# Attention with a gated MLP on one core: early first keys, 64-row pairs, and the output copy on VectorE

## Chip, core and metric

One of the eight cores of a Trainium2 chip. The metric is device time in microseconds of one execution. Engines: TensorE (PE; its weight loads are PEld), VectorE (DVE), ScalarE (ACT), GpSimd (POOL) and SyncE (SP, which here only issues DMAs).

## The reference

```python
xn  = layernorm(A_x)                             # (2048, 512)
q, k, v = split(xn @ A_wqkv)                     # 32 heads of 16
p   = softmax(q @ k.T * 16**-0.5, axis=-1)       # 32 x 2048 x 2048
s   = concat(p @ v) @ A_wo
g   = silu(gelu(xn @ B_w1 + B_b1) @ B_w2 + B_b2) # hidden 1376
out = A_x + s * g
```

## The kernel before

Projections and MLP are made of two-part numbers: every float32 operand is split into a rounded high part and the rest, and a product takes three matmuls (high x high, high x low, low x high). q and k go out to DRAM as qk_h and qk_l and come back in the layout of the scores. A group is 4 heads (8 groups); a unit is one group and one chunk of 512 queries (32 units, u = 4 x group + chunk).

TensorE runs most matmuls as row tiles: a matmul that contracts over 64 rows or fewer takes rows 0 to 63 or 64 to 127 of the array, and two of them, one in each row tile (the code's `a` is 0 or 1), run at once. All instructions are placed by hand; each engine takes its own in the order of the program.

Softmax needs the row maximum before the exponential. So each unit is scored twice. An **S tile** (`s_mm`, L178) is 128 queries x 512 keys of one head into a PSUM bank, and VectorE takes its maxima (`s_max`, L184); 64 of them make a unit, 2,048 in all, and behind a unit come a reduce over its maxima (nm, L239), a split on GpSimd and a transpose (mh, L258) that goes to DRAM. A **T tile** (`t_one`, L710) is 128 keys x 512 queries, with the maxima as two more rows of the contraction, and ScalarE's exponential (L712) carries it to SBUF. A **V** (`pv_step`, L775) multiplies the four heads' exponentials of 128 keys with v, into the one bank of `ps_v`, over 16 steps of a unit; then the bank is copied to `os` (L782) and moved, divided and used.

The **first part** (to about 476 us) computes layernorm, q, k and v, and the MLP. At its start, transposes (`turn`, L422), v tiles (`v_tile`, L79) and the q and k of groups 0 and 1 (`q_first`, L438) are full-array matmuls of 128 rows. From 52 us on everything runs in `run()` (L561) as pairs of 64 rows, one in each row tile. `fill()` puts S tiles between them once row `FILL0` of this counting is reached, spread evenly over the rows: 4 x `LEAD` = 576 of them. S tiles alternate between the banks `ps_a` and `ps_b`.

The **second part** runs 512 steps, 16 to a unit; step n makes the T tiles of step n and the V of step n-1:

```python
ORDER = {0: "TTTTV", 3: "TSXTTSTYV"}
def due(n):
    return min(4 * L, 4 * LEAD + max(0, 3 * n - 1))
```

The difference of `due` is the number of S tiles in a step: three till they run out, at n = 491, and none afterwards. X and Y are two half tiles, one in each row tile, that share a bank: X (256 keys) is written first, a token through the POOL queue (L216) tells that it is done, then Y follows and one maximum covers both. S tiles use three banks here (`ps_a`, `ps_b`, `ps_x`), T tiles four. From n = 492 the output projections of finished tokens run in the steps as well.

Keys lie in three buffers (`KB`, group g in buffer g % 3): one from the start (kt0), one where v's weights were (kt1), one in two of the slots of the normalized x. The keys of group 0 come in by chunks (`load_k`) when kt0 is free, the queries of unit 0 and 1 by `load_qs` into qz0 and qz1.

Of the kernel before, what the change touches and what calls it, by code (L numbers as in the profile page):

```python
# [8 lines left out]
F32 = mybir.dt.float32  # L9
# [7 lines left out]
P = 128  # L17
# [12 lines left out]
EPS = 1e-5  # L30
SCALE = DH ** -0.5
VW = DH + 1
LEAD = 144
NW = 10
EARLY = 4
DONE = 492
FILL0 = 38
HB = 4
W2B = 2
ORDER = {0: "TTTTV", 3: "TSXTTSTYV"}  # L40
HC = CH // 2
KB = 3
XB = 6
BANKS = ("ttvt", "xtmt", "ttvt")

# [2 lines left out]
def fused(ctx: ExitStack, tc: tile.TileContext, x, wqk, wv, wo, w1, b1, w2, b2, out):  # L48
# [50 lines left out]
        return src[r0:r0 + 48, c0:c0 + n].rearrange("(p d) s -> d p s", d=DH)[:, 0:3:2, :]  # L99

    def load_k(g, pieces=range(6), eng=nc.sync, c0=0, n=S):
        both = kws[g % KB]
        for i in pieces:
            a, b = divmod(i, 3)
            r, cs = slice(64 * a + DH * b, 64 * a + DH * b + DH), slice(c0, c0 + n)
            src = rows((qk_h, qk_h, qk_l)[b], g, 1, a, c0, n)
            if both is not None:
                eng.dma_start(both[r, :, cs].bitcast(F32), src)
            else:
                for p in range(2):  # L110
                    eng.dma_start(kts[g % KB][p][r, cs].bitcast(F32), src[:, p])

    def k_ones(kt):
        for p in range(2):
            for a in range(2):
                nc.sync.dma_start(kt[p][64 * a + 48:64 * a + 50].bitcast(F32), ones_d)

    def new_k(pool):
        both = pool.tile([P, 2, S], F32R, name=f"kt{len(kts)}")
# [46 lines left out]

    def at_of(job):
        u, st, p = job
        return divmod(st, NCH) if u % (NCH * KB) else divmod(st, NCH)[::-1]

    def s_mm(ps, job, a, c0, k0, w):
        u, st, p = job
        qi, ki = at_of(job)
        if u not in MX:
            MX[u] = qring.tile([P, GH, NCH, NCH, 2], F32, name="mx")
        r = slice(64 * a, 64 * a + 3 * DH)
        k0 += ki * CH
        return nc.tensor.matmul(ps[:, c0:c0 + w], QS[u][r, p, qi * P:(qi + 1) * P],  # L178
                                kts[u // NCH % KB][p][r, k0:k0 + w], start=True, stop=True).ins

    def s_max(ps, job, heads, parts):
        u, p = job[0], job[2]
# [81 lines left out]
    xh = [slot(2 * c, (P, KT, CH), F32R) for c in range(NCH)]  # L264
    xl = [slot(2 * c + 1, (P, KT, CH), F32R) for c in range(NCH)]
    wk = sa.enter_context(tc.tile_pool(name="work_a", bufs=2))
    b1_sb = xp.tile([P, FT], F32, name="b1_sb")
    b2_sb = xp.tile([P, D], F32, name="b2_sb")

# [102 lines left out]
    with ExitStack() as s1:  # L372
# [126 lines left out]
        for c in range(1, NCH):  # L499
            for t in range(NCH * c, NCH * c + NCH):  # L500
                turn(t)
            if c < NCH - 1:
                ln(NCH * c + NCH, NCH)
            else:
                nc.scalar.activation(warm[:, 1:], warm[:, :1], AF.Gelu_apprx_tanh)
                w1_load(0)
                w2_load(0)
                w2_load(1)
                break
            v_tile(c - 1)  # L510
            q_first(c)

    keep_r = ctx.enter_context(tc.tile_pool(name="keep_r", bufs=1, side="right"))
    qring = ctx.enter_context(tc.tile_pool(name="qring", bufs=2, side="right"))
# [6 lines left out]
    for i in range(2):  # L521
        qzs.append(qzp.tile([P, 2, CH], F32R, name=f"qz{i}"))

    load_qs(0)
    load_k(0, c0=0, n=CH)
    load_k(0, c0=CH, n=S - 2 * CH)
    v_tile(NCH - 2)
    q_first(NCH - 1)
    v_tile(NCH - 1)
    load_k(0, c0=S - CH, n=CH)  # L530

    prog.update(n=0, pe=0, seen=0)
    writer = {}
    s_when, row = [], [0, 0]
    ndown = sum(1 for e in plan if e[0] == "down")
    ROWS = 12 * (4 * VQ + 2 * len(pairs)) + 6 * ndown - 10 + 2 * LEAD - FILL0

    def fill(a):
        due = FILL0 + sum(made) * ROWS // (4 * LEAD)
# [53 lines left out]

    PH = {}

    def terms(u, a, begin):
        kind, n, f = u
        c = f if kind == "q" else n
        out = []
        for k in range(KT):  # L600
            for i, j in ((0, 0), (0, 1), (1, 0)):
                if kind == "v":
                    lhs, rhs = (xh, xl)[i][c][:, k, f * P:(f + 1) * P], (wv_h, wv_l)[j][:, k]
                else:
                    w = W1[u if kind == "m" else n]
                    lhs, rhs = w[i][:, k * P:(k + 1) * P], (xh, xl)[j][c][:, k]
                out.append([u, PH[u], lhs, rhs, False, False])
        if begin:
            out[0][4] = True
        else:  # L610
            out[-1][5] = True
        return out
# [3 lines left out]
    def down(c, f, part):  # L616
        i = c * FT + f
        if f == 0 and part == 0:
            PA[c] = [ps_v.tile([P, D], F32, name="pv")] + [ps_t.tile([P, D], F32, name="pst") for t in range(3)]
        h, w = HS[c, f], W2[c, f]  # L620
        side = (part + i) % 2
        ops = [[], []]
        for a in range(2):
            for t in ((0, 1), (2, 3))[(a + side) % 2]:
                ts = slice(t * P, (t + 1) * P)
                for n, (x, y) in enumerate(((0, 0), (0, 1), (1, 0))):
                    ops[a].append(((c, t), PA[c][t], h[x][:, ts], w[y],
                                   f == 0 and part == 0 and n == 0, f == FT - 1 and part == 1 and n == 2))
        n = prog["pe"]
        if (c, f, part) == parts[-2]:  # L630
            run(ops, {2: [lambda: mark(True)], 5: [lambda: mark(True)]})
        else:
            run(ops, {3: [lambda: mark_early(n)]})
        if part == 0:
            w2_split(i + 1)
            w2_load(i + 3)
            return
        del HS[c, f], W2[c, f]
        if f == FT - 1:
            for t in (0, 2, 1, 3):  # L640
                gt = wk.tile([P, D], F32, name="gt", bufs=4)
                if c == NCH - 1:
                    nc.vector.tensor_add(gt, PA[c][t], b2_sb)  # L643
                else:
                    nc.scalar.activation(gt, PA[c][t], AF.Copy)
                rs = slice(c * CH + t * P, c * CH + (t + 1) * P)
                if c < NCH - 1:
                    chores.append((gt, rs))
                else:
                    nc.gpsimd.dma_start(g_d[rs, :], gt)  # L650
# [22 lines left out]
    def quad(n, at):  # L673
# [4 lines left out]
        for i in range(at, at + 2):  # L678
# [4 lines left out]
            if i >= 2:  # L683
                for u in (us[i - 2], us[i]):
                    v_out(u[1] * NCH + u[2], PH.pop(u))

    def ask_k(g):
        errands.append((k_ones, kts[g]))
        for i in range(6):
            errands.append((load_k, g, (i,)))  # L690
# [12 lines left out]
    def t_one(u, k, p, a):  # L703
        g = u // NCH
        if (u, k) not in PT:
            PT[u, k] = slot(3 + len(PN) % 3, (P, GH, CH))
            PN.append(1)
        ps = t_tile()
        r = slice(64 * a, 64 * a + 3 * DH + 2)
        nc.tensor.matmul(ps, kts[g % KB][p][r, k * P:(k + 1) * P],  # L710
                         QT[u][r, p, :], start=True, stop=True)
        nc.scalar.activation(PT[u, k][:, 2 * p + a, :], ps, AF.Exp, scale=SCALE)  # L712

    k_ones(kts[0])
    for n, e in enumerate(plan):
        if e[0] == "half":
            half(*e[1:])
        elif e[0] == "first":
            quad(*e[1:])
            if e[1:] == (0, 2):  # L720
                ask_qs(1)
        else:
            if e[1] == parts[-2]:
                nc.scalar.activation(mhw, ident_r[:1, :1].bitcast(F32), AF.Exp)
            if e[1] == parts[-1]:
                for i in range(EARLY):
                    t_one(0, 0, i // 2, i % 2)
            down(*e[1])
# [21 lines left out]
    qts.append(kp.tile([P, 2, CH], F32R, name="qt1"))  # L750
    load_qt(1)
    load_mh(1)
    wo_h = kp.tile([P, KT, D], F32R, name="wo_h")
    wo_l = kp.tile([P, KT, D], F32R, name="wo_l")

    WR = {}

# [11 lines left out]
    def pv_step(u, k):  # L769
# [8 lines left out]
        if k == NT - 1:  # L778
            OS[u] = wb.tile([P, CH], F32, name="os", bufs=1)
            pv = PV.pop(u)  # L780
            if u < NU - 1:
                nc.scalar.activation(OS[u], pv, AF.Copy)  # L782
            else:
                nc.scalar.activation(OS[u][:, :HC], pv[:, :HC], AF.Copy)
                nc.vector.tensor_copy(OS[u][:, HC:], pv[:, HC:])
# [29 lines left out]

    def home(i):
        if i not in homes:
            homes[i] = (slot(i, (P, KT, D)) if i < KB else
                        keep_r.tile([P, 2 * KT, D], F32, name="kt0"))
        return homes[i]  # L820

    def load_gx(t):
# [1 line left out]
        if t < NW and i < 6:  # L824
            GX[t] = wb.tile([P, 2, D], F32, name="gx", bufs=3)
        elif t < NT - NCH:
            GX[t] = home(KB)[:, i - 6 * (t < NW):][:, :2]
        else:
            GX[t] = home(1 + i // KT)[:, i % KT:i % KT + 2]
        nc.sync.dma_start(GX[t][:, 0], g_d[t * P:(t + 1) * P, :])  # L830
# [78 lines left out]
    L = 16 * NU  # L909

    def due(n):
        return min(4 * L, 4 * LEAD + max(0, 3 * n - 1))

    for u in range(NU):
        g, c = divmod(u, NCH)
        if c == 0 and g == KB:
            for i in range(6):
                at(56 + i, load_k, g, (i,), nc.gpsimd, 0, S // 2)
                at(64 + i, load_k, g, (i,), nc.gpsimd, S // 2, S // 2)
        elif c == 0 and g > KB:  # L920
            for i in range(6):
                at(64 * (g - KB + 1) + 6 + i, load_k, g, (i,), nc.gpsimd)
        if u >= 2:
            at(16 * u - 14, load_qt, u)
            need = min(n for n in range(L) if due(n) >= 64 * (u + 1)) + (4 if u < NU - 1 else 2)
# [22 lines left out]
    for i, t in enumerate(late[:2]):  # L948
        at(L - 2 + i, w_token, t)
    for k in range(KT):  # L950
        at(104 + 16 * k, load_wo, k)
        at(110 + 16 * k, wo_high, k)
        at(114 + 16 * k, wo_low, k)
    jobs.extend(heads[made[0]:])
    for n in range(L + 1):
        ua, ka = divmod(n, 16)
# [73 lines left out]
```

## Time and profile before

| | |
|---|---|
| median of 3 runs | 1575.72 us (1575.42 to 1576.03) |
| the profiled execution | 1575.59 us |
| its span, first to last instruction | 1573.8 us, granted clock 0.999 |
| first part, 64-row pairs | 52.56 to 475.6 us |
| first V group of the second part | 477.27 us |
| steps with output projections | from about 1475 us |

In the page, busy time is the union of an engine's instructions; "mean ns" is that of one. The chain of waits follows the end of the program backwards through what released each instruction. A timeline row is a start, a length, engine, line, operation, output and inputs, and a count when neighbours of one kind are merged into a row (the length is then from the first start to the last end); in brackets stands what the engine was idle for.

### The profile page before, as it was taken

What the parts mean: (1) busy time and instruction counts of PE and PEld (TensorE: products, weight loads), DVE (VectorE), ACT (ScalarE), POOL (GpSimd) and SP (SyncE); (2) the same over time, 40 slices, a digit from 0 to 9 for tenths busy, and PEclk for the clock granted to TensorE, in tenths of its full rate; (3) what the DMA queues carried; (4) which work ended last, traced back from release to release, by engine and by line L of the source; (5) the groups of instructions that cost most, each with busy time, mean ns of one, the idle gap of its engine ahead of it and who ended that gap; (6) DMA issues with size and microseconds to landing.
All of it is one profiled execution on the core that took longest, in us unless ns stands there. A gap on an engine that the chain in (4) does not pass through costs nothing.

```text
span 1573.8 us, 32597 instructions
## 1 busy us (share of the span) xinstructions
PE 1561.6 (99%) x12234; PEld 955.1 (61%) x12234; DVE 1376.2 (87%) x2275; ACT 1254.8 (80%) x2516; POOL 378.0 (24%) x398
## 2 busy tenths in 40 slices
PE   8999999999999999999999999999999999999998
PEld 7899999999995444444444444444444444444455
DVE  7499999999998999999999999999999999999733
ACT  4333433434339999999999999999999999999994
POOL 4135575765641001001100200000010000000144
PEclk9999999999999999999999999999999999999999
DMA  6625442454422114111511411221041111111162
GB/s 208 152 60 141 130 139 99 134 155 123 132 84 76 43 30 72 30 36 36 86 31 31 69 37 36 52 51 29 23 79 30 33 29 31 41 29 23 45 210 100
DMA packets 79486, 116.92 MB, mean 74 GB/s; under 512 B 28868, under 2 KB 29124, under 8 KB 78152
## 3 DMA queue, kind: packets, MB, share of 16 engines
q1 hardware_dynamic: 75580, 101.90, 23.9%
q0 software_dynamic: 3264, 12.35, 4.1%
q8 instruction: 96, 1.57, 0.4%
q10 hardware_dynamic: 484, 0.60, 0.1%
q14 instruction: 62, 0.51, 0.1%
HBM read 84.35 MB, written 25.97 MB: 70 GB/s over the span
## 4 chain that ended last, share of the span: by engine, by line
PE 98%; DVE 1%; issue 0%; DMA 0%; ACT 0%; POOL 0%; DVEq 0%
PE pv L775 33%; PE pst L710 16%; PE ps L710 14%; PE ps L561 13%; PE ps L178 9%; PE pst L561 7%; PE pv L561 2%; PE ps L881 1%; PE ps L438 1%; PE ps L79 1%; PE pst L79 1%; DVE st L399 0%; PE pst L422 0%; DMA xt<-in_x 0%; PE pst L438 0%
## 5 line engine op out<-in xcount | busy, mean ns | idle before, releaser
L184 DVE TENSOR_REDUCE mx<-ps 128x2 f32<-128x512 f32 x2048 | 1299.2, 685 | 129.8 <-PE ps L178 46.7
L712 ACT ACTIVATE slot<-pst 128x512 f32<-128x512 f32 x1533 | 809.5, 616 | 2.1 <-PE ps L710 0.8
L775 PE MATMUL pv<-slot,vsb 128*17 128x512 f32 (+1 forms) x4096 | 539.2, 599 | 0.0
L178 PE MATMUL ps<-kt,slot 48*128 48x512 f32 x1364 | 383.8, 370 | 1.1 <-POOLq L216 1.1
L712 ACT ACTIVATE slot<-ps 128x512 f32<-128x512 f32 x515 | 311.7, 606 | 5.6 <-PE ps L710 3.6
L710 PE MATMUL pst<-qt,kt 50*128 50x512 f32 x1149 | 311.4, 406 | 0.5 <-DVE gt L643 0.3
L710 PEld LDWEIGHTS ps<-qt,kt 50*128 50x128 f32 x387 | 70.7, 183 | 323.6 <-ACT slot L712 322.7
L710 PEld LDWEIGHTS pst<-qt,kt 50*128 50x128 f32 x1149 | 212.1, 185 | 29.7 <-ACT slot L712 11.0
L178 PEld LDWEIGHTS ps<-kt,slot 48*128 48x128 f32 x1364 | 225.4, 184 | 3.1 <-POOLq L216 1.4
L561 PE MATMUL ps<-slot,w1h 64*128 64x512 f32 x1088 | 217.7, 394 | 0.0
L178 PE MATMUL ps<-kt,qz 48*128 48x512 f32 x512 | 213.0, 416 | 0.0
L710 PE MATMUL ps<-qt,kt 50*128 50x512 f32 x387 | 190.8, 495 | 0.0
L178 PE MATMUL ps<-slot,slot 48*128 48x512 f32 x598 | 167.9, 369 | 0.0
L561 PEld LDWEIGHTS ps<-slot,w1h 64*128 64x128 f32 x1088 | 150.4, 186 | 8.6 <-ACT junk L575 2.7
L561 PE MATMUL ps<-slot,w1l 64*128 64x512 f32 x544 | 141.2, 392 | 0.0
L358 POOL TENSOR_TENSOR hl<-hg,hh 128x512 fp32r<-128x512 f32 x76 | 96.8, 1296 | 135.6 <-ACT hh L357 67.2
L575 ACT ACTIVATE junk<-ident_r 1x1 f32<-1x1 f32 x92 | 18.0, 196 | 126.7 <-PE pst L561 118.5
L775 PEld LDWEIGHTS pv<-slot,vsb 128*17 128x17 f32 (+1 forms) x4096 | 69.1, 96 | 81.7 <-issue 23.9
L178 PEld LDWEIGHTS ps<-kt,qz 48*128 48x128 f32 x512 | 93.9, 183 | 16.0 <-DVE mx L184 0.6
L710 PE MATMUL pst<-qt,slot 50*128 50x512 f32 x384 | 102.4, 407 | 0.0
L178 PEld LDWEIGHTS ps<-slot,slot 48*128 48x128 f32 x598 | 98.9, 184 | 0.9
L242 POOL CAST nmh<-nm 128x16 fp32r<-128x16 f32 x32 | 6.3, 197 | 353.6 <-PE pst L710 176.4
(151 smaller groups left out, 1756.7 us busy)
## 6 DMA issues: line engine op xcount, KB each, us to landing
raw<-in_w SPq DMA_DIRECT2D x88, 256.0 KB
qk_h<-hh SPq DMA_DIRECT2D x32, 256.0 KB
qk_l<-hl SPq DMA_DIRECT2D x32, 256.0 KB
qt<-qk_h SPq DMA_DIRECT2D x128, 64.0 KB
slot<-qk_h SPq DMA_DIRECT2D x92, 64.0 KB
g_d<-gt POOLq DMA_DIRECT2D x16, 256.0 KB, 3.3
qt<-qk_l SPq DMA_DIRECT2D x64, 64.0 KB
dn<-den_d SPq DMA_DIRECT2D x128, 32.0 KB
```

The lines of the kernel that those rows point to most:

```text
L79: nc.tensor.matmul(ps, lhs[a], rhs[b], start=first and n == 0, stop=last and n == 2)
L178: return nc.tensor.matmul(ps[:, c0:c0 + w], QS[u][r, p, qi * P:(qi + 1) * P], kts[u // NCH % KB][p][r, k0:k0 + w], start=True, stop=True).ins
L184: nc.vector.tensor_reduce(MX[u][:, 2 * p:2 * p + 2, qi, ki][:, heads, parts], ps.rearrange("p (n c) -> p n c", c=HC), axis=AX.X, op=OP.max)
L242: nc.gpsimd.tensor_copy(hl[:, 0], nm)
L358: nc.gpsimd.tensor_sub(hl, raw, hh.bitcast(F32))
L438: nc.tensor.matmul(pq["q", g, c], W1[g][i][:, k * P:(k + 1) * P], (xh, xl)[j][c][:, k], start=n == 0 and k == 0, stop=n == 2 and k == KT - 1)
L561: i = nc.tensor.matmul(ps, lhs[r], rhs[r], start=first, stop=last).ins
L575: i = nc.scalar.activation(junk[:, :1], ident_r[:1, :1].bitcast(F32), AF.Copy).ins
L710: nc.tensor.matmul(ps, kts[g % KB][p][r, k * P:(k + 1) * P], QT[u][r, p, :], start=True, stop=True)
L712: nc.scalar.activation(PT[u, k][:, 2 * p + a, :], ps, AF.Exp, scale=SCALE)
L775: nc.tensor.matmul(PV[u][32 * j:32 * j + w, :], vsb[:, k, h:h + w], PT[u, k][:, j, :], start=(k == 0), stop=(k == NT - 1))
L881: op = nc.tensor.matmul(PW[b][0], OTS[b, k][i][r], (wo_h, wo_l)[j][r, k], start=part == 0 and n == 0, stop=part == 3 and n == 5).ins
```

## The change

- Constants: `LEAD` 144 to 151 (604 early S tiles instead of 576), `FILL0` 38 to 13.
- Two-tile steps: `due` lets one tile out each 16 steps from n = 50 on; such a step has S, S and no X and Y ("TSTTSTV").
- The copy of pv to `os` at a unit's end goes from ScalarE to VectorE (except that of the last unit, as before split between the two).
- The v tiles 2 and 3 and the q and k of chunk 3 leave the full-array section. `pairs_first` makes them as four runs of 64-row pairs, with S tiles between.
- Keys of group 0, chunk 0, are loaded early into a tile of their own, `k_first`, and the queries of unit 0 into another (both have the space of the `gt` tiles, which are made later as two of double size). `load_first` issues these loads behind the q and k of chunk 1. Unit 0 reads `k_first` for its first 16 S tiles. Chunk 0 of the buffer kt0 is loaded later, with chunk 3 and unit 1's queries.
- A fourth key buffer: groups 0 to 7 use buffers 0, 1, 2, 3, 0, 2, 1, 0 and are loaded at other steps; `wo_h` and `wo_l` take the fourth buffer's space after group 3, and late output tiles kt1's instead of kt0's.

```diff
-LEAD = 144
+LEAD = 151
...
-FILL0 = 38
+FILL0 = 13
...
-ORDER = {0: "TTTTV", 3: "TSXTTSTYV"}
+ORDER = {0: "TTTTV", 2: "TSTTSTV", 3: "TSXTTSTYV"}
+LIGHT = 34
-KB = 3
+KSET = (0, 1, 2, 3, 0, 2, 1, 0)
+KAT = {3: 4, 4: 70, 5: 198, 6: 262, 7: 326}
...
+    def load_first():
+        for i in range(6):
+            a, b = divmod(i, 3)
+            r = slice(64 * a + DH * b, 64 * a + DH * b + DH)
+            nc.sync.dma_start(k_first[r].bitcast(F32), rows((qk_h, qk_h, qk_l)[b], 0, 1, a, 0, CH))
+        q_rows(QS[0], 0)
...
-        return divmod(st, NCH) if u % (NCH * KB) else divmod(st, NCH)[::-1]
+        return divmod(st, NCH) if u else divmod(st, NCH)[::-1]
...
+        if u or ki:
+            keys = kts[KSET[u // NCH]][p][r, k0 + ki * CH:][:, :w]
+        else:
+            keys = k_first[r, p, k0:k0 + w]
...
+    k_first, QS[0] = [wk.tile([P, 2, CH], F32R, name="gt") for i in range(2)]
...
             q_first(c)
+            if c == 1:
+                load_first()
...
-    load_qs(0)
-    load_k(0, c0=0, n=CH)
     load_k(0, c0=CH, n=S - 2 * CH)
-    v_tile(NCH - 2)
-    q_first(NCH - 1)
-    v_tile(NCH - 1)
-    load_k(0, c0=S - CH, n=CH)
...
-    ROWS = 12 * (4 * VQ + 2 * len(pairs)) + 6 * ndown - 10 + 2 * LEAD - FILL0
+    ROWS = 12 * (4 + 4 * VQ + 2 * len(pairs)) + 6 * ndown - 10 + 2 * LEAD - FILL0
...
+    def pairs_first():
+        v2 = [("v", 0, NCH - 2), ("v", 0, NCH - 1)]
+        q2 = [("q", g, NCH - 1) for g in range(2)]
+        for u, (pool, name) in zip(v2 + q2, ((ps_v, "pv"), (ps_m, "ps"), (ps_x, "ps"), (ps_t, "pst"))):
+            PH[u] = pool.tile([P, CH], F32, name=name)
+        run((terms(v2[0], 0, True), terms(v2[1], 1, True)))
+        run((terms(q2[0], 0, True, True), terms(q2[1], 1, True, True)), {6: [mark]})
+        run((terms(v2[1], 0, False), terms(v2[0], 1, False)), {6: [mark]})
+        for u in v2:
+            v_out(u[2], PH.pop(u))
+        run((terms(q2[1], 0, False), terms(q2[0], 1, False)))
+        evac(q2, PH)
+        load_k(0, c0=S - CH, n=CH)
+        load_k(0, c0=0, n=CH)
+        load_qs(1)
...
+    pairs_first()
     k_ones(kts[0])
...
-            if e[1:] == (0, 2):
-                ask_qs(1)
...
-    wo_h = kp.tile([P, KT, D], F32R, name="wo_h")
-    wo_l = kp.tile([P, KT, D], F32R, name="wo_l")
+    new_k(kp)
+    wo_h, wo_l = [kws[3][:, i].rearrange("p (k d) -> p k d", d=D) for i in range(2)]
...
-                nc.scalar.activation(OS[u], pv, AF.Copy)
+                nc.vector.tensor_copy(OS[u], pv)
...
-        return min(4 * L, 4 * LEAD + max(0, 3 * n - 1))
+        return min(4 * L, 4 * LEAD + max(0, 3 * n - 1 - max(0, (n - LIGHT) // 16)))
...
-        if c == 0 and g == KB:
+        if c == 0 and g in KAT:
+            if g == 3:
+                at(KAT[g] - 1, k_ones, kts[KSET[g]])
             for i in range(6):
-                at(56 + i, load_k, g, (i,), nc.gpsimd, 0, S // 2)
-                at(64 + i, load_k, g, (i,), nc.gpsimd, S // 2, S // 2)
-        elif c == 0 and g > KB:
-            for i in range(6):
-                at(64 * (g - KB + 1) + 6 + i, load_k, g, (i,), nc.gpsimd)
+                at(KAT[g] + i, load_k, g, (i,), nc.gpsimd)
...
-        at(104 + 16 * k, load_wo, k)
+        at(266 + 16 * k, load_wo, k)
```

`terms(u, a, begin, late)` gains an order for `late`: all terms with the high part of x before those with its low part.

More of the change, by code (lines that the diff above doesn't have):

```diff
@@ L101, in load_k @@
     def load_k(g, pieces=range(6), eng=nc.sync, c0=0, n=S):
-        both = kws[g % KB]
+        both = kws[KSET[g]]
         for i in pieces:
@@ L110, in load_k @@
                 for p in range(2):
-                    eng.dma_start(kts[g % KB][p][r, cs].bitcast(F32), src[:, p])
+                    eng.dma_start(kts[KSET[g]][p][r, cs].bitcast(F32), src[:, p])
     def k_ones(kt):
@@ L176, in s_mm @@
         r = slice(64 * a, 64 * a + 3 * DH)
-        k0 += ki * CH
-        return nc.tensor.matmul(ps[:, c0:c0 + w], QS[u][r, p, qi * P:(qi + 1) * P],
-                                kts[u // NCH % KB][p][r, k0:k0 + w], start=True, stop=True).ins
+        if u or ki:
+            keys = kts[KSET[u // NCH]][p][r, k0 + ki * CH:][:, :w]
+        else:
+            keys = k_first[r, p, k0:k0 + w]
+        return nc.tensor.matmul(ps[:, c0:c0 + w], QS[u][r, p, qi * P:(qi + 1) * P], keys, start=True, stop=True).ins
     def s_max(ps, job, heads, parts):
@@ L594, in fused, with terms @@
     PH = {}
-    def terms(u, a, begin):
+    def terms(u, a, begin, late=False):
         kind, n, f = u
@@ L599, in terms @@
         out = []
[L600 to L607, printed above, removed]
+        order = [(k, i, j) for k in range(KT) for i, j in ((0, 0), (0, 1), (1, 0))]
+        if late:
+            order = [(k, i, j) for i, j in ((0, 0), (1, 0), (0, 1)) for k in range(KT)]
+        for k, i, j in order:
+            if kind == "v":
+                lhs, rhs = (xh, xl)[i][c][:, k, f * P:(f + 1) * P], (wv_h, wv_l)[j][:, k]
+            else:
+                w = W1[u if kind == "m" else n]
+                lhs, rhs = w[i][:, k * P:(k + 1) * P], (xh, xl)[j][c][:, k]
+            out.append([u, PH[u], lhs, rhs, False, False])
         if begin:
@@ L639, in down @@
         if f == FT - 1:
-            for t in (0, 2, 1, 3):
-                gt = wk.tile([P, D], F32, name="gt", bufs=4)
+            both = [wk.tile([P, 2, CH], F32R, name="gt") for i in range(2)]
+            for n, t in enumerate((0, 2, 1, 3)):
+                gt = both[n // 2][:, n % 2].bitcast(F32)
                 if c == NCH - 1:
@@ L709, in t_one @@
         r = slice(64 * a, 64 * a + 3 * DH + 2)
-        nc.tensor.matmul(ps, kts[g % KB][p][r, k * P:(k + 1) * P],
+        nc.tensor.matmul(ps, kts[KSET[g]][p][r, k * P:(k + 1) * P],
                          QT[u][r, p, :], start=True, stop=True)
         nc.scalar.activation(PT[u, k][:, 2 * p + a, :], ps, AF.Exp, scale=SCALE)
+    pairs_first()
     k_ones(kts[0])
@@ L817, in home @@
         if i not in homes:
-            homes[i] = (slot(i, (P, KT, D)) if i < KB else
-                        keep_r.tile([P, 2 * KT, D], F32, name="kt0"))
+            homes[i] = (slot(i, (P, KT, D)) if i < 3 else
+                        keep_v.tile([P, 2 * KT, D], F32, name="kt1"))
         return homes[i]
@@ L826, in load_gx @@
         elif t < NT - NCH:
-            GX[t] = home(KB)[:, i - 6 * (t < NW):][:, :2]
+            GX[t] = home(3)[:, i - 6 * (t < NW):][:, :2]
         else:
@@ L950, in fused @@
     for k in range(KT):
-        at(104 + 16 * k, load_wo, k)
-        at(110 + 16 * k, wo_high, k)
-        at(114 + 16 * k, wo_low, k)
+        at(266 + 16 * k, load_wo, k)
+        at(272 + 16 * k, wo_high, k)
+        at(276 + 16 * k, wo_low, k)
     jobs.extend(heads[made[0]:])
```

## The prediction

> **What bounds the kernel now.** I read the page first, then busy time by stretches, the chain of waits in order of time, and the timeline engine by engine around one unit boundary.
>
> ```profile
> PE 1561.6 (99%) x12234; PEld 955.1 (61%) x12234; DVE 1376.2 (87%) x2275; ACT 1254.8 (80%) x2516; POOL 378.0 (24%) x398
> ...
> 40.00:60.00 20.00, 20.00 (x128) 16.27 (x127) 3.22 (x6) 8.39 (x16) 5.09 (x4) 1.00 0.71 172
> ...
> 52.56:475.60 423.04, 423.04 (x3558) 387.25 (x3557) 373.94 (x596) 159.93 (x358) 238.90 (x209) 1.00 0.42 121
> ...
> 900.00:1000.00 100.00, 100.00 (x780) 47.55 (x773) 92.79 (x153) 99.80 (x198) 4.67 (x7) 1.00 0.13 30
> ```
>
> The first line is the whole span. The other three are stretches (length, then busy time and count of PE, PEld, DVE, ACT and POOL, then granted clock, DMA share, GB/s). From 40 to 60 us VectorE does 3.22 us of work while TensorE is full; in the first part it is busy 88% (373.94 of 423.04), in the second 93%, and there ScalarE shows 99.8% too. Busy time can't say which of the two holds the second part, so I took the starts of the V groups (eight pv matmuls, one group a step) from the chain of waits, and one boundary in the timeline.
>
> ```profile
> 873.00 1.07 PE pv L775 x8
> 875.39 1.05 PE pv L775 x8
> ...
> 905.91 1.07 PE pv L775 x8
> 908.29 1.05 PE pv L775 x8
> ```
> ```profile
> 901.78 1.05 PE L775 MATMUL pv<-slot,vsb 128*17 128x512 f32 x8
> ...
> 903.81 1.05 PE L775 MATMUL pv<-slot,vsb 128*17 128x512 f32 x8
> 904.79 0.49 PE L710 MATMUL ps<-qt,kt 50*128 50x512 f32 x1
> ...
> 905.13 0.40 PE L710 MATMUL pst<-qt,kt 50*128 50x512 f32 x1
> 905.14 0.28 PE L178 MATMUL ps<-kt,slot 48*128 48x256 f32 x1
> 905.25 0.40 PE L710 MATMUL pst<-qt,kt 50*128 50x512 f32 x1
> 905.36 0.41 PE L178 MATMUL ps<-kt,slot 48*128 48x512 f32 x1
> 905.49 0.42 PE L710 MATMUL pst<-qt,kt 50*128 50x512 f32 x1
> ...
> 905.91 1.07 PE L775 MATMUL pv<-slot,vsb 128*32 128x512 f32 x8
> ```
> ```profile
> 901.76 1.57 ACT L712 ACTIVATE slot<-pst 128x512 f32<-128x512 f32 x3
> 905.22 0.63 ACT L782 ACTIVATE os<-pv 128x512 f32<-128x512 f32 x1
> 906.18 1.64 ACT L712 ACTIVATE slot<-pst 128x512 f32<-128x512 f32 x3
> ```
>
> A normal step is 2.03 us (901.78 to 903.81). ScalarE's part: three exponentials take 1.57, one alone about 0.60, so one more costs (1.57-0.60)/2 = 0.49 and four cost 1.96. ScalarE has 0.07 a step to spare; TensorE sets the step. Not at a boundary: the copy of pv (L782, 0.49 more) puts ScalarE behind by 0.42, and TensorE waits, 2.10 from 903.81 to 905.91 and 2.38 from 905.91 to 908.29. A unit is 905.91-873.00 = 32.91 us = 14x2.03 + 2.10 + 2.38, so **a boundary costs 0.42**. Where VectorE's nm reduce (L239, once per 64 S tiles) lands between two row maxima, a step is longer too.
>
> ```profile
> 566.18 0.28 DVE L239 TENSOR_REDUCE nm<-mx 128x16 f32<-128x128 f32 x1
> ...
> 566.07 1.05 PE L775 MATMUL pv<-slot,vsb 128*17 128x512 f32 x8
> ...
> 568.26 1.05 PE L775 MATMUL pv<-slot,vsb 128*17 128x512 f32 x8
> ```
>
> That step is 2.19: a VectorE instruction of 0.28 in the wrong place costs 0.16, since the next S matmul waits for its bank.
>
> **The copy moves to VectorE, with a two-tile step behind it.**
>
> ```profile
> 61.80 0.69 DVE L184 TENSOR_REDUCE mx<-ps 128x2 f32<-128x512 f32 x1 [17.35 <-PE ps L178]
> ...
> 903.34 3.91 DVE L184 TENSOR_REDUCE mx<-ps 128x2 f32<-128x512 f32 x6
> 907.47 1.29 DVE L184 TENSOR_REDUCE mx<-ps 128x2 f32<-128x512 f32 x2 [0.22 <-PE ps L178]
> ...
> L643 DVE TENSOR_TENSOR gt<-pst,b_sb 128x512 f32<-128x512 f32 x3 | 1.9, 678 | 0.0
> ...
> L785 DVE COPY os<-pv 128x256 f32<-128x256 f32 x1 | 0.4, 424 | 1.0 <-ACT os L784 1.0
> ```
>
> Two maxima back to back take 1.29, one 0.69 (the first row is the first of all), so VectorE starts one every 0.60 and three take 1.80 of 2.03. No full copy of PSUM by VectorE is in this trace: between 0.42 (the half copy) and 0.75 (a tenth above the add), I take 0.68, the add that reads the same 128x512 from PSUM. In the boundary step the maxima start at 903.34, 903.94 and 904.54, so the copy starts at 905.14 (pv is ready at 904.86) and ends at 905.82. The next V is due at 903.81+2.03 = 905.84 and now starts near 905.87 instead of 905.91. What queues behind the copy: the next step's three maxima, which then start at 905.74, 906.34 and 906.94 and end at 906.43, 907.02 and 907.62. With three tiles in the step after, its second S (905.36 plus one V interval, 2.03 to 2.06, so 907.4) takes the bank of the third maximum and waits for 907.62: 0.25 to 0.3. In a two-tile step no X takes a bank, so that S gets the bank that came free at 907.02 and hardly waits; VectorE catches up there (two maxima, 1.2 of 1.9 us).
>
> Without X and Y each row tile of TensorE loses 256 columns: X at 905.14 to the next instruction of its row tile at 905.25 is 0.11 to 0.12. The light step is then 1.91 on TensorE; ScalarE's 1.96 may hold it at that, so I take 1.95. Three intervals at a boundary go from 2.10+2.38+2.03 = 6.51 to 2.04+1.95+2.03 = 6.02: 0.49 less, of which 0.42 is the copy. Light steps are those at which (n-34)//16 grows with tiles left, n = 50 to 482: 28, all right behind a copy. 28x0.49 = 13.7. Boundaries 0 and 1 (n = 16, 32) have no light step: 2.04+2.35 against 4.48, 0.09 each, 0.2. Against it, the nm reduces: 47 tiles to a unit instead of 48 let them drift against the steps. I reckon with some 12 collisions at 0.16 and four that meet the copy at 0.2, 2.7 us, against about 8x0.16 = 1.3 now: +1.4. **Second part: -12.5** (a copy of 0.75 would make it -10.5, one of 0.6 -12.6).
>
> The Trainium skill speaks against this edit: "Advanced Engine Details and Errata", The Read-Write Bubble, advises that ScalarE is closer to PSUM and VectorE closer to SBUF, to be used accordingly. The rows agree on the price: 0.60 on VectorE against 0.49 on ScalarE. If that 0.11 lay on the path at 30 boundaries the sum would be 3.3 us worse. By the rows it doesn't: VectorE has 0.23 a step free, ScalarE 0.07.
>
> **64-row pairs and early keys.**
>
> ```profile
> 41.27 3.00 PE L79 MATMUL ps<-kt,slot 128*128 128x512 f32 x12
> ...
> 52.56 0.49 PE L561 MATMUL pst<-kt,slot 64*128 64x512 f32 x1
> ...
> 53.36 0.39 PE L561 MATMUL pst<-kt,slot 64*128 64x512 f32 x1
> ...
> 53.58 0.39 PE L561 MATMUL pst<-kt,slot 64*128 64x512 f32 x1
> ```
>
> Forty-eight full-array matmuls fill 41.27 to 52.56, 11.29 us, with no S beside them. They become 48 pairs, and 28 more S tiles are 14 more rows (a row is one 64- or 48-row matmul in each of the two row tiles). Before, 1,488 rows of pairs and 288 of S (3,552 of the 3,558 matmuls of that stretch) took 423.0 us: 0.238 a row; without S a row is 0.228 (53.36 to 53.58 and the like). New: 62 rows x 0.238 = 14.8, and 25 rows fewer run without S, +0.3. 14.8+0.3-11.3 = **+3.8**. The maxima per row stay as they were (1,728 rows to 576, now 1,815 to 604), so VectorE isn't loaded more densely; it starts near 44.5 instead of 61.80. What lets 28 more tiles in is this start. The 28 tiles gone from the second part are the light steps above, counted there.
>
> Do the early loads land in time?
>
> ```profile
> 33.47 0.32 SPq L364 DMA_DIRECT2D qk_l<-hl  x1
> ...
> 40.95 0.32 SPq L363 DMA_DIRECT2D qk_h<-hh  x1
> ...
> 46.65 0.33 SPq L133 DMA_DIRECT2D qz<-qk_h  x1
> ...
> 38.00:42.00 4.00, 4.00 (x27) 3.36 (x26) 2.62 (x9) 3.27 (x7) 0.94 (x1) 1.00 0.08 24
> ...
> 46.00:50.00 4.00, 4.00 (x19) 3.24 (x18) 0.00 (x0) 0.63 (x2) 0.00 (x0) 1.00 1.04 272
> ...
> 58.00:62.00 4.00, 4.00 (x38) 3.31 (x36) 0.20 (x1) 1.09 (x3) 0.00 (x0) 1.00 1.09 128
> ...
> 43.76 0.68 DVE L74 TENSOR_TENSOR slot<-ps,slot 128x512 fp32r<-128x512 f32 x1
> ```
>
> load_first puts 12 DMAs on SP's queue behind the chunk 1 outputs (last issue 33.47). The next thing SP has to issue is at 40.95, and from 38 to 42 the DMA engines are 8% busy: at 0.33 to twice that each (46.65's row) the 12 are out by 38 to 42, and the first S, in row 14 (41.27+13x0.228 = 44.2), finds them landed. Its bank is one that a turn uses until VectorE's split ends at 44.44: +0.2, in TensorE's program order, so everything behind it waits too. The first 16 S tiles live on k_first. The 17th needs chunk 1 of keys, three rows a tile, in row 61 or so: 44.2+48x0.238 = 55.7. The load of the middle chunks goes out where qz's did, from 46.65, behind weight loads that keep the DMA engines full to 50; its 0.79 MB (six DMAs of 32 rows of 4 KB) at the 128 GB/s seen from 58 to 62, where the same load ran, is 6.1 us: landing near 55 to 56. I price the wait at 0.5, between 0 and 5 (if the load ran only when it did before, to 62). The chunk 0 and 3 loads and load_qs(1) follow the last q outputs on SP; tile 49 needs chunk 3 in row 157 (78 us), tile 65 the rest in row 205 (90 us): the cover is 15 us and more, and costs nothing. **First part: +3.8+0.2+0.5 = +4.5.**
>
> ```profile
> kt<-qk_h POOLq DMA_DIRECT2D x12, 256.0 KB, 5.5
> ```
>
> At no cost: the fourth key buffer (the keys of group 3 are issued by POOL at n = 4 to 9 and read from about n = 55; behind POOL's issue waits the token between X and Y, as it does now at steps 70 and on), wo in that buffer once group 3 is through at n = 256 (read first at 492), gx in kt1, whose last group ends at n = 448. Were one of these late, a step would wait for such a DMA (5.5 us, this row), once.
>
> **Sum.** -12.5+4.5 = -8.0. The profiled execution took 1575.59 us (span 1573.8 and 1.8 around it), the median of the runs is 0.13 more: 1575.7-8.0 = **1567.7 us**.
>
> **Rivals.** (A) *VectorE takes ScalarE's place.* If the copy delays the S banks as the nm reduce does, ahead of the maxima and not behind, its 0.60 costs 0.60-0.12 = 0.48 at each of 30 boundaries: +14.4, 1582. From 0.27 a boundary the gain is gone, from 0.37 the kernel is measurably slower. For it: VectorE is 93% busy and 0.28 us cost 0.16 once. Against it: the copy waits for pv at 904.86 and two of the step's maxima have started by then, and the two-tile step follows at once. (B) *The early S tiles wait for keys.* In-order TensorE then stands at tile 17, by up to 5 us: 1572.7. For it: DMA engines full from 46 to 50. Against: before, this load queued behind 12 others. (C) *ScalarE is the second part's bound*, and light steps give no more than 0.07: 28x0.05 is already in; if they give nothing, -8.0+28x0.08 = 1570. (D) *The two-tile steps come to nothing since TensorE's stall moves to the T banks*: the last exponential of a step must end before the next T on its bank, 0.13 us of room now (901.76+1.57+2.03 = 905.36 against 905.49); 28x0.1 more, 1570.5 as well.
>
> **Numbers.** Forecast 0.66, C and D together 0.10, B 0.10, A 0.14 in various degrees. The range takes in the low ends (first part +3, no collisions, light steps at 1.91: 1563) and a third of A or all of B: 1563 to 1574. A difference within 0.2% (3.2 us) is about what a measurement of this kernel can't tell from none. Forecast, C, D and most of B give faster, 0.82; the rest of B and A where it is weak give same, 0.08; A in full gives slower, 0.10.
>
> **What would show it.** V starts 2.03 to 2.06 apart across a boundary, then 1.91 to 1.96, and units of 32.4 us instead of 32.9; L782's copies on DVE at 0.68; first maximum near 44.5 and the first pv group about 4.5 us later than now; ScalarE below 99.8%. Wrong if boundary intervals stay at 2.3 or more with the S matmul after the copy waiting on DVE, if TensorE idles before tile 17, or if the first part is longer by over 6 us.

## Result and the profile after

The changed kernel takes **1569.27 us** (median of 5 runs, 1569.08 to 1570.00) against 1575.72 before: ratio 0.9961, 95% interval 0.9949 to 0.9972. It is 6.45 us faster; 8.0 were forecast. The span went from 1573.8 to 1567.4.

The page's first line and busy time by stretches, as before:

```profile
PE 1556.5 (99%) x12254; PEld 956.3 (61%) x12254; DVE 1390.5 (89%) x2306; ACT 1244.5 (79%) x2487; POOL 375.3 (24%) x392
```
```profile
40.00:60.00 20.00, 20.00 (x170) 17.59 (x170) 16.73 (x27) 8.42 (x17) 5.08 (x4) 1.00 0.74 197
...
900.00:1000.00 100.00, 99.84 (x785) 47.46 (x778) 93.25 (x157) 99.60 (x197) 5.60 (x10) 1.00 0.13 34
```

From 40 to 60 us VectorE now works 16.73 instead of 3.22 us. In the second part hardly anything shows: ScalarE 99.60 for 99.80. The gain is read from starts. The first V group, in the timeline:

```profile
480.31 1.07 PE L801 MATMUL pv<-slot,vsb 128*32 128x512 f32 x8
```

That is 480.31 against 477.27: the first part is **3.04 longer** (4.5 forecast). From this V group to the one of step 481, 480 steps on, it is 979.56 us against 988.69: **9.13 less** (12.5 forecast). The rest, steps with output projections and the tail, is 0.3 shorter.

One lit boundary (with a two-tile step behind it) in the timeline, TensorE, VectorE and ScalarE:

```profile
1033.97 1.05 PE L801 MATMUL pv<-slot,vsb 128*17 128x512 f32 x8
...
1036.04 1.06 PE L801 MATMUL pv<-slot,vsb 128*32 128x512 f32 x8
1037.04 0.50 PE L737 MATMUL ps<-qt,kt 50*128 50x512 f32 x1
1037.04 0.50 PE L190 MATMUL ps<-slot,slot 48*128 48x512 f32 x1
1037.38 0.72 PE L737 MATMUL pst<-qt,kt 50*128 50x512 f32 x3
1037.61 0.39 PE L190 MATMUL ps<-slot,slot 48*128 48x512 f32 x1
1038.03 1.05 PE L801 MATMUL pv<-slot,vsb 128*17 128x512 f32 x8
...
1039.70 0.49 PE L737 MATMUL pst<-qt,kt 50*128 50x512 f32 x1
...
1040.12 0.62 PE L801 MATMUL pv<-slot,vsb 128*17 128x512 f32 x4
```
```profile
1035.30 0.68 DVE L808 COPY os<-pv 128x512 f32<-128x512 f32 x1
1035.90 2.48 DVE L195 TENSOR_REDUCE mx<-ps 128x2 f32<-128x512 f32 x4
1038.29 0.28 DVE L250 TENSOR_REDUCE nm<-mx 128x16 f32<-128x128 f32 x1
```
```profile
1035.98 1.57 ACT L739 ACTIVATE slot<-pst 128x512 f32<-128x512 f32 x3
1037.57 0.60 ACT L739 ACTIVATE slot<-ps 128x512 f32<-128x512 f32 x1
1038.07 1.57 ACT L739 ACTIVATE slot<-pst 128x512 f32<-128x512 f32 x3
```

The copy on VectorE takes 0.68 and ends at 1035.98; the V behind it starts at 1036.04, 2.07 after the one before, so 0.04 late. ScalarE's pile is gone. The light step takes 1.99 and the next 2.09: three intervals of 6.15 instead of 6.50 (the median over units 3 to 29 is 6.14, before 6.50). The boundary is nearly free now, but the light step, the one with two tiles, saves nothing: 1.99+2.09 is two normal steps of 2.03 and 0.02.

Apart from the first step and the boundaries, seventeen steps are now 2.18 to 2.25 long (about 0.15 or more over a normal one), where before there were six (and one of 2.12). The nm reduce stands in 14 of them; two more come just behind a boundary at which nm met the copy, and one shows no nm. Boundaries 0 and 1, which have no light step, take 2.34 where lit ones take 1.99.

### The profile page after: what moved, and what is told of

Its sections match the earlier page's. It is cut to its first block, busy times and chain, and to the rows that moved or that the text cites. A ratio compares the mean times of both kernels' runs of the same rounds, so it can differ in the third digit from the quotient of the medians.

```text
span 1567.4 us, 32580 instructions
## 1 busy us (share of the span) xinstructions
PE 1556.5 (99%) x12254; PEld 956.3 (61%) x12254; DVE 1390.5 (89%) x2306; ACT 1244.5 (79%) x2487; POOL 375.3 (24%) x392
## 4 chain that ended last, share of the span: by engine, by line
PE 98%; DVE 1%; DMA 0%; issue 0%; ACT 0%; POOL 0%; DVEq 0%
PE pv L801 32%; PE pst L737 15%; PE ps L737 14%; PE ps L569 13%; PE ps L190 10%; PE pst L569 7%; PE pv L569 3%; PE ps L907 1%; PE ps L450 1%; PE ps L81 1%; PE pst L81 1%; DVE st L411 0%; PE pst L434 0%; DMA xt<-in_x 0%; DVE slot L76 0%; DVE xn L425 0%
## 5 line engine op out<-in xcount | busy, mean ns | idle before, releaser
L739 ACT ACTIVATE slot<-ps 128x512 f32<-128x512 f32 x515 | 307.7, 598 | 7.2 <-PE ps L737 4.6
L737 PE MATMUL pst<-qt,kt 50*128 50x512 f32 x1149 | 304.3, 405 | 0.5 <-DVE gt L654 0.3
L569 PE MATMUL ps<-slot,w1h 64*128 64x512 f32 x1104 | 222.8, 393 | 0.0
L737 PEld LDWEIGHTS pst<-qt,kt 50*128 50x128 f32 x1149 | 207.4, 185 | 22.0 <-DVE gt L654 1.1
L190 PE MATMUL ps<-kt,qz 48*128 48x512 f32 x448 | 187.0, 418 | 0.0
L569 PEld LDWEIGHTS ps<-slot,w1h 64*128 64x128 f32 x1104 | 156.1, 185 | 5.0 <-ACT junk L583 0.2
L569 PE MATMUL ps<-slot,w1l 64*128 64x512 f32 x552 | 145.6, 392 | 0.0
L838 POOL TENSOR_TENSOR slot<-slot,dn 64x512 f32<-64x512 f32 x16 | 20.5, 1282 | 312.4 <-PE pst L737 176.6
L190 PEld LDWEIGHTS ps<-kt,qz 48*128 48x128 f32 x448 | 82.0, 183 | 15.4 <-DVE mx L195 1.0
```

Source lines behind the costliest of these rows:

```text
L569: i = nc.tensor.matmul(ps, lhs[r], rhs[r], start=first, stop=last).ins
L737: nc.tensor.matmul(ps, kts[KSET[g]][p][r, k * P:(k + 1) * P], QT[u][r, p, :], start=True, stop=True)
L838: eng.tensor_mul(ot[c][rs, g // 2], ot[c][rs, g // 2], DN.pop(u)[rs])
```

## Experiments

**The two edits of the second part, one by one.** Theory 1: they only work together; a light step shortens nothing, it makes room on VectorE behind the copy. Theory 2: their effects add, and a light step is worth 0.08 to 0.12 by itself. (The expectation calls theory 2 the prediction's. That is so for the light step's own 0.08; but the prediction also had the room, since it put a boundary with the copy moved and no light step at 2.04+2.35.) A copy on ScalarE again:

```diff
-                nc.vector.tensor_copy(OS[u], pv)
+                nc.scalar.activation(OS[u], pv, AF.Copy)
```

> The changed kernel with the copy of pv back on ScalarE, the two-tile steps kept. Theory 1 (the two edits work only together: a two-tile step saves no time by itself, since the last T of the step waits for ScalarE; it only makes room on VectorE): boundaries cost 0.42 as in the kernel before, V starts 2.10 and 2.38 apart, units of about 32.9 us, time 1579 (1578.3 to 1579.8). Theory 2 (the effects add, as the prediction had them: 0.08 to 0.12 us a two-tile step, whoever copies): units of 32.8 us, 1575.5 to 1577.

No light steps (`LIGHT = 9999`):

> The changed kernel with three tiles in every step until they run out (n = 482), the copy on VectorE. Theory 1: the second S of the step after the copy's waits for the bank of the maximum that queues behind the copy, as at boundaries 0 and 1 of the changed kernel (2.34 instead of 2.00): 28 boundaries x 0.25 = +7.0, minus 0.4 for nine more steps without S: 1575.9 (1574.8 to 1576.8). Theory 2: only the two-tile steps' own 0.12 is lost: 1569.3+3.3 = 1572.6.

Both:

> The changed kernel with the copy on ScalarE and no two-tile steps: what is left is the first part's edit with 604 early tiles. Both theories: the first V group 3.0 later than before, the second part as before but for nine more steps without S (0.05 to 0.1 each): 1578.2 (1577.5 to 1578.7). It is the base for the two edits: with it the copy alone (no two-tile steps) is worth 2.3 and the two-tile steps alone nothing or -0.8 by theory 1, 9 and 3 by theory 2.

No light steps and `LEAD = 144`:

> The changed kernel with 576 early tiles instead of 604 and no two-tile steps, the copy on VectorE. Theory 1: 14 rows less in the first part, -3.2 us there against the run without two-tile steps; the 28 tiles come back in nine steps of the second part that ScalarE holds at nearly the same length, +0.5: 1573.2. Theory 2: a tile costs TensorE the same 0.12 in either part: no difference to the run without two-tile steps, 1572.6 if that is 1572.6.

Measured ("480 steps": from the first V group to that of step 481; "boundary": mean of the three intervals around it from unit 3 on):

| | time, us | first V | 480 steps | boundary |
|---|---|---|---|---|
| before | 1575.75 | 477.27 | 988.69 | 2.09+2.38+2.02 |
| neither edit, 604 early tiles | 1579.30 | 480.91 | 989.87 | 2.10+2.39+2.02 |
| light steps alone, copy on ScalarE | 1579.68 | 480.84 | 989.60 | 2.10+2.38+2.02 |
| copy on VectorE alone | 1576.63 | 480.21 | 987.35 | 2.06+2.34+2.02 |
| both (the changed kernel) | 1569.27 | 480.31 | 979.56 | 2.07+1.99+2.08 |
| copy on VectorE alone, 576 early tiles | 1572.01 | 476.07 | 986.22 | 2.06+2.34+2.02 |

The ratios to before are 1.0022 (1.0013 to 1.0032), 1.0024 (1.0015 to 1.0034), 1.0006 (0.9996 to 1.0016) and 0.9976 (0.9966 to 0.9986) for the four new ones in the table's order.

Theory 2 falls. Over the 480 steps light steps alone are worth 0.3 us, the copy's move alone 2.5, both 10.3: 7.5 us belong to neither. (The run with neither edit came out 1.1 above its expectation: the first V group, at 480.9, was 0.6 later than in the changed kernel, and the 480 steps have 15 long ones instead of six. The run with 576 tiles came out 1.2 below theory 1's 1573.2, for one thing because the 28 tiles cost 4.1 in the first part and not 3.2.) The light steps aren't free: they need the 28 tiles, which put the first V group from 476.07 to 480.21. Against the copy alone with 576 tiles the changed kernel is only 2.7 us faster (1569.27 against 1572.01). The copy alone, in the timeline of the run without light steps, TensorE, then one of its weight loads, then VectorE:

```profile
1039.85 1.06 PE L801 MATMUL pv<-slot,vsb 128*32 128x512 f32 x8
1040.84 0.50 PE L737 MATMUL ps<-qt,kt 50*128 50x512 f32 x1
...
1041.31 0.39 PE L737 MATMUL pst<-qt,kt 50*128 50x512 f32 x1
1041.64 0.50 PE L190 MATMUL ps<-slot,slot 48*128 48x512 f32 x1
1041.65 0.50 PE L737 MATMUL pst<-qt,kt 50*128 50x512 f32 x1
...
1042.19 1.05 PE L801 MATMUL pv<-slot,vsb 128*17 128x512 f32 x8
```
```profile
1041.64 0.18 PEld L190 LDWEIGHTS ps<-slot,slot 48*128 48x128 f32 x1 [0.27 <-DVE mx L195]
```
```profile
1039.11 0.68 DVE L808 COPY os<-pv 128x512 f32<-128x512 f32 x1
1039.71 3.76 DVE L195 TENSOR_REDUCE mx<-ps 128x2 f32<-128x512 f32 x6
```

The second S starts at 1041.64, 0.33 after the T before it; at the boundary shown in the prediction it was 0.11 (905.25 to 905.36). Its weight load waits 0.27 for a maximum: the third behind the copy starts at 1039.71+2x0.60 = 1040.91 and ends at 1041.59. That is the wait worked out in the prediction as 0.25 to 0.3, and it takes nearly the whole place of ScalarE's pile: 2.34 for 2.38.

**What holds the light step?**

```diff
-        nc.scalar.activation(PT[u, k][:, 2 * p + a, :], ps, AF.Exp, scale=SCALE)
+        w = CH - P if (p, a) == (1, 0) and "seen" not in prog else CH
+        nc.scalar.activation(PT[u, k][:, 2 * p + a, :w], ps[:, :w], AF.Exp, scale=SCALE)
+        if w < CH:
+            nc.gpsimd.memset(PT[u, k][:, 2 * p + a, w:], 1.0)
```

> The changed kernel, where in the second part the last exponential of each step is computed for 384 of its 512 columns and GpSimd fills the others with 1: ScalarE has 0.12 less a step (1.84 instead of 1.96). Left out is a sixteenth of the exponentials. If the two-tile steps are held by ScalarE (the last T of the step waits for the exponential of the last T before, on its bank): their interval falls from 1.99 to 1.91, and the next, now 2.08, to 2.03 to 2.05, 28 x 0.11 = 3 us less, about 1566. If TensorE itself needs 1.99 (two full tiles end together before V): they stay at 1.99 and 2.08, and the time within 1 us of 1569.3.

Measured, in one run: 1565.37 us, the 480 steps 975.74. The same boundary, TensorE and one of its weight loads; ScalarE; and ScalarE's semaphore instructions of this line from 480 to 1470 us:

```profile
1033.74 1.06 PE L804 MATMUL pv<-slot,vsb 128*32 128x512 f32 x8
1035.69 1.05 PE L804 MATMUL pv<-slot,vsb 128*17 128x512 f32 x8
1037.77 0.62 PE L804 MATMUL pv<-slot,vsb 128*17 128x512 f32 x4
```
```profile
1037.34 0.18 PEld L737 LDWEIGHTS pst<-qt,kt 50*128 50x128 f32 x1
```
```profile
1035.33 0.60 ACT L740 ACTIVATE slot<-ps 128x512 f32<-128x512 f32 x1
1035.82 1.47 ACT L740 ACTIVATE slot<-pst 128x512 f32<-128x512 f32 x3
```
```profile
L740 ACTq EVENT_SEMAPHORE  x485: 17/17/17, 486.3 to 1469.7; - x162
```

The light step is 1.95 (median 1.945), the next stays at 2.08, and normal steps got 0.01 shorter, from 2.030 to 2.022, which is most of the 3.8 us (390 steps x 0.008 = 3.1). So the expectation was half right. The weight loads tell what holds these steps. In the changed kernel, at the boundary of the result above:

```profile
1037.04 0.18 PEld L737 LDWEIGHTS ps<-qt,kt 50*128 50x128 f32 x1 [0.84 <-ACT slot L739]
...
1039.69 0.18 PEld L737 LDWEIGHTS pst<-qt,kt 50*128 50x128 f32 x1 [0.15 <-ACT slot L739]
```

The last T of a step takes the bank of the last T of the step before, which the fourth exponential of that step frees. That one ends at 1038.07+1.57 = 1039.64, and the weight load starts 0.05 later, at 1039.69. So there is a chain over two steps, from a V to the second V after it: V to the first T, first T to its exponential, four exponentials, last T of the next step, V. Over the light step and the next one it is, as a mean of 26 boundaries, 0.99+0.53+2.07+0.05+0.43 = 4.07, and the two intervals are 1.99+2.08. The S, X and Y of a step don't appear in it, so leaving out X and Y can't make it shorter: what a light step gains the next gives back.

In the run with shorter exponentials the last T of the next step still waits for the fourth exponential (1035.82+1.47 = 1037.29, weight load at 1037.34): 0.99+0.59+1.96+0.05+0.43 = 4.02, against 1.94+2.08. The exponentials are 0.11 shorter, but 0.06 of that is lost before the first of them: since GpSimd now writes a part of the same tile, the edit has put a semaphore instruction ahead of each step's first exponential (485 of them; the changed kernel has none there). So the chain through ScalarE holds the light step and the next one together, and nothing shows a part of the 1.99 that is TensorE's own.

The same chain holds normal steps. In the kernel before, a weight load of the last T starts 0.05 to 0.06 behind the end of that exponential in 303 of the 312 steps counted in the middle of units, and the five parts are 0.98+0.53+2.07+0.05+0.43 = 4.06, twice 2.03. At a boundary of that kernel the copy on ScalarE stands ahead of the first exponential, which starts 0.90 behind the first T instead of 0.53: 0.98+0.90+2.12+0.05+0.43 = 4.48, which is 2.10+2.38. This also says why light steps alone gave nothing.

**The long steps.**

```diff
-        if ended:
+        if ended and "seen" in prog:
             s_end0(ended.pop())
...
+            late = ended[:]
             s_max(ps, job, slice(0, 2), n)
+            if late:
+                s_end0(ended.pop(0))
             s_ring.append(pool)
```

> The changed kernel, where in the second part the nm reduce of a finished S unit is put behind the maximum of the next Y instead of behind the next maximum of any kind. If the 17 long steps (2.18 to 2.25 us) come from nm between two maxima of one step: they go, 17 x 0.17 = 2.9 us less, 1566.4 (1566 to 1567.3). If they come from something else at a unit's end of S (the GpSimd split, the transpose): they stay, 1569.3.

Measured: 1567.22 us (1566.85 to 1567.49), ratio to before 0.9947 (0.9934 to 0.9959). Long steps: 5 instead of 17, the 480 steps 977.68 instead of 979.56, the first V group 0.19 later. So 12 of 17 came from where nm stands in VectorE's queue; four of the five left are at two boundaries, where nm meets the copy. This kernel is faster than the one before and than the changed one.

**The first part: what the early start is worth.** `FILL0 = 88`, and later `FILL0 = 50`:

> The changed kernel with FILL0 = 88: the same rows, the same 604 early tiles, but the first S tile at about 62 us as in the kernel before, so one tile every 2.88 rows instead of 3.00. If the early start is what lets the 28 more tiles in (VectorE would otherwise be too full): maxima come every 0.68 us, VectorE falls behind, TensorE waits for the two S banks, the first V group 3 us or more later than 480.3. If TensorE alone sets the first part: the first V group at 480.3 to 481.0 and 1569.3 to 1570.0 in all; the early keys would then be worth nothing as such.

> The changed kernel with FILL0 = 50: the first S tile near 53 us, one tile every 2.94 rows. If a floor of about 0.72 us per S tile (VectorE with two S banks) already holds the first part, as (496.2-62.1)/604 = 0.719 in the run with FILL0 = 88 suggests: the first V group at 53+604x0.719 = 487. If the floor is not reached before 2.9 rows a tile: 480.3 to 482.

Measured: 1585.30 us (ratio 1.0062, 1.0047 to 1.0077), first V group at 496.21, which is 15.9 later; and, in one run, 1577.58, first V group at 488.37 (487 expected). The maxima in the first 474 us, by their line: count, shortest, median and longest in ns, then first and last start. Before, changed, FILL0 = 50, FILL0 = 88, and 576 tiles with the early start:

```profile
L184 DVE TENSOR_REDUCE mx<-ps x576: 648/687/694, 61.8 to 472.6; 128x2 f32<-128x512 f32 x192
```
```profile
L195 DVE TENSOR_REDUCE mx<-ps x601: 649/691/694, 45.0 to 473.2; 128x2 f32<-128x512 f32 x151
```
```profile
L195 DVE TENSOR_REDUCE mx<-ps x590: 648/690/694, 53.7 to 473.8; 128x2 f32<-128x512 f32 x197
```
```profile
L195 DVE TENSOR_REDUCE mx<-ps x579: 647/685/694, 62.1 to 473.7; 128x2 f32<-128x512 f32 x193
```
```profile
L195 DVE TENSOR_REDUCE mx<-ps x576: 647/691/694, 45.1 to 471.2; 128x2 f32<-128x512 f32 x192
```

410.8/575 = 0.714 us a tile, then 0.714, 0.713 and 0.712, whatever the plan asks for (3.00, 3.00, 2.94 and 2.88 rows a tile); only 576 tiles with the early start, with a plan of 3.13 rows, come more slowly, 0.741 apart. There is **a floor of 0.713 us a tile**, and start plus tiles times floor gives the end of the first part: 16.8 us earlier, 28 tiles more, 28x0.713-16.8 = 3.2 against 3.04 measured. The kernel before and the changed one both stand where this floor and TensorE's rows meet. Where the floor is from, a stretch of the run with FILL0 = 88 shows, VectorE and one weight load of an S tile:

```profile
200.86 2.67 DVE L195 TENSOR_REDUCE mx<-ps 128x2 f32<-128x512 f32 x4 [0.17 <-PE pst L569]
203.71 2.69 DVE L195 TENSOR_REDUCE mx<-ps 128x2 f32<-128x512 f32 x4 [0.18 <-PE ps L569]
```
```profile
203.59 0.18 PEld L190 LDWEIGHTS ps<-kt,qz 48*128 48x128 f32 x1
```

Four maxima take 2.67, 0.18 more than back to back (3x0.60+0.69 = 2.49), and 0.18 pass before the next four. With two banks, an S tile can only start when the maximum before the last is through, and then VectorE waits for it: the first row ends at 200.86+2.67 = 203.53, and the S's weight load starts 0.06 later. In this run 559 of the first 568 S tiles counted start like that, 0.05 to 0.065 behind that maximum, in the kernel before 553, and with 576 tiles and the early start only 414. What a third bank would give is open: none is free in the first part.

**More light steps.** nm behind Y as above, `LIGHT = -14`, `LEAD = 152`:

> The kernel with nm behind Y, and a two-tile step behind every copy (n = 2, 18, 34 and on, and a last one at 491) with 608 early tiles. Boundaries 0 and 1 go from 2.34 to about 2.00: -0.6. Four more early tiles: +0.6 if TensorE sets the first part (0.15 a tile), +2.9 if the floor of 0.72 a tile does. In all 1567.2, or 1569.5.

Measured: 1568.91 us, ratio 0.9958 (0.9945 to 0.9972). The 480 steps took 976.75, 0.93 less than with nm behind Y alone (0.6 expected; two long steps are left instead of five), the first V group came at 483.05 instead of 480.50: +2.55, or 0.64 for each of four tiles. That is near the floor's price and far from the 0.15 of TensorE.

**A split copy.** 576 early tiles, no light steps, nm behind Y, and the two halves on two engines as at the last boundary:

```diff
-            if u < NU - 1:
-                nc.vector.tensor_copy(OS[u], pv)
-            else:
+            if True:
                 nc.scalar.activation(OS[u][:, :HC], pv[:, :HC], AF.Copy)
                 nc.vector.tensor_copy(OS[u][:, HC:], pv[:, HC:])
```

> 576 early tiles, no two-tile steps, nm behind Y, and the copy of pv split at every boundary as at the last: 256 columns by ScalarE, 256 by VectorE. By theory 1 a half copy costs each engine about half of 0.49 and 0.60: ScalarE is 0.25-0.07 = 0.18 behind, the third maximum after the copy 0.27 earlier than with the whole copy, so that the S bank is free in time: boundaries cost 0.1 to 0.2 instead of 0.37 (whole copy, no two-tile step), and the first V group comes at 476.1 as with 576 tiles: 1572.0-30x0.2-1.3 = 1564.7, between 1563.5 and 1568. If half a copy on each engine makes both late: 1570 and more.

Measured: 1579.60 us (ratio 1.0025, 1.0015 to 1.0035), 14.9 above the 1564.7 of theory 1 and 7.6 more than with the whole copy on VectorE and nm in its old place. Boundaries are 2.34+2.34+2.02. Its timeline, VectorE and ScalarE:

```profile
1038.60 0.42 DVE L812 COPY os<-pv 128x256 f32<-128x256 f32 x1 [0.45 <-ACT os L811]
```
```profile
1038.15 0.41 ACT L811 ACTIVATE os<-pv 128x256 f32<-128x256 f32 x1
```

VectorE waits 0.45 for ScalarE's half to end (1038.15+0.41 = 1038.56): the halves run one after the other, and the wait stands in VectorE's queue. The group of L785 quoted in the prediction shows it already for the last boundary ("1.0 <-ACT os L784").

## Why the prediction was right, and where not

- **The copy.** 0.68 was taken, 0.68 measured; V starts 0.04 late (0.03 forecast); the wait at boundaries without a light step, 0.25 to 0.3 forecast, makes 2.34 there (2.35 forecast). The light step takes this wait away as worked out. Rival A had the copy delay S banks at all 30 boundaries. The run without light steps shows such a delay, at 0.31 (2.34-2.03) and not 0.48: 7.4 us with the same early tiles. That run is no faster than before, but not only for this: its 28 early tiles cost 4.1 us in the first part, and with 576 tiles the copy alone is 3.7 faster than before, 1.2 of it in the first part.
- **What sets the step was misread, and the light step's own gain with it.** "ScalarE has 0.07 a step to spare; TensorE sets the step" compared ScalarE's 1.96 with one step; the chain of the experiments spans two, 4.06, and leaves nothing to spare. The 1.95 and 2.03 that were taken are 1.99 and 2.08. At 6.14 instead of 6.02 for three intervals, 28 boundaries give 3.4 us less. Rival D had this mechanism, the last T waiting for its bank, and C its engine; together they were given 0.10, and only for the light step and not the one after it. Their 1570 and 1570.5 lie nearer to the result than the forecast. D was held off by 0.13 us of room, the exponential's end (905.36) against the T (905.49). That T's weight load, in the kernel before, shows that there was no room; it starts 0.06 after the end, 903.79+1.57 = 905.36:

```profile
905.42 0.18 PEld L710 LDWEIGHTS pst<-qt,kt 50*128 50x128 f32 x1
```
```profile
903.79 1.57 ACT L712 ACTIVATE slot<-pst 128x512 f32<-128x512 f32 x3
```

- **nm collisions.** +1.4 was forecast for 16 against eight; 17 were measured against six, 0.175 and 0.166 each: 17x0.175-6x0.166 = +2.0. Twelve behave as the prediction says and four stand at or just behind two boundaries where nm meets the copy, also as forecast.
- **The first part.** 3.04 against +4.5. There was no wait for keys (0.5 taken, rival B): the 17th S tile, the first on kt, starts at 55.87, 55.7 forecast.

```profile
55.28 0.41 PE L190 MATMUL ps<-gt 48*128 48x512 f32 x1
...
55.87 0.42 PE L190 MATMUL ps<-kt,gt 48*128 48x512 f32 x1
```

  The row count came out near the mark (+3.8 without the waits), but its parts did not. The 28 tiles cost 4.1 (3.3 forecast), and the rest of the edit, with 576 tiles, made the first part 1.2 shorter (476.07 against 477.27) where the count had it 0.4 longer; the two errors partly cancel, which is luck. No run undoes the 64-row pairs or the early keys by themselves, so the 1.2 isn't split between them. The reason behind the count was incomplete too. "VectorE isn't loaded more densely" is true and was treated as a side condition; it is what decides. Had the start not been early, the same rows would have cost 15.9 us more.
- **ScalarE against VectorE.** The Trainium skill's advice ("Advanced Engine Details and Errata", The Read-Write Bubble) that ScalarE is closer to PSUM and VectorE closer to SBUF agrees with the prices, 0.49 against 0.60. It didn't decide: the copy alone on VectorE is 2.5 us faster over the 480 steps, and with room made 10.3.

The forecast of 1567.7 lay 1.6 below the result: it had the light steps and the collisions about 4 us too good, the first part 1.5 too bad, and smaller terms make up the rest. That errors of both signs met is why it came so close. The fourth key buffer, put at no cost, shows none: apart from the first step and the boundaries no step of the 480 is longer than 2.25.

## What to carry to other kernels

Moving work from a full engine to one that is nearly full moves the wait unless room is made at that very place: here neither the move (2.5 us) nor the room (0.3) was worth much alone, and both were worth 10.3. Price such pairs together, with what the room costs elsewhere (4.1 in the first part), and follow the chain over as many steps as it spans before a shorter step is booked as a gain. Whether an engine waits is read from the weight load that starts when a bank comes free, not from the matmul behind it. When one engine consumes at a floor rate, the moment its stream starts counts like its length; and a small instruction between two of a tight queue is worth moving by one place (1.9 us over 480 steps here).

## What the runs showed of the hardware

- A matmul whose weight load was held and starts only with it is recorded at 0.49 to 0.50, others of its form at 0.39 (1039.69 and 1039.70; 1041.64 against 1041.31).
- A weight load that waits for a bank starts about 0.05 after the instruction that frees it ends (1039.64 and 1039.69; 1041.59 and 1041.64).
- Two banks and one VectorE let through one 128x512 maximum per 0.713 us, though two back to back take 0.60 from start to start.
